# A fourth place for finished row blocks, and stores in the order of their results

## The chip, the cores and the metric

The kernel runs on one core of a Trainium2 chip. The metric is the device time of one execution in microseconds (us); the median of three executions stands for a kernel. The profile is that of one further execution, so its span is a little apart from the median. TensorE multiplies matrices, VectorE (DVE), ScalarE (ACT) and GpSimd (POOL) do the element-wise work, and SyncE (SP) issues all transfers.

## The reference

With x of 2048 rows by 512 columns, the result is a gated mixture of two branches, one gate per row:

```python
g = _sigmoid((x * gate_w).sum(-1, keepdims=True))
a = _A_ref(x, A_wqkv, A_wo)          # 32 heads of 16, causal, window of 256 rows, then @ wo
b = _B_ref(x, B_w1, B_b1, B_w2, B_b2)
return g * a + (1 - g) * b
```

Branch B works across the rows: `h = layernorm(x)`, `u = gelu(h^T w1 + b1)` with 1376 hidden columns, `y = u w2 + b2`, transposed back to 2048 by 512. Everything is bf16.

## The kernel before

The 2048 rows are 16 blocks of 128. The kernel is a list of small named tasks, each with the engines that may run it, the tasks it depends on and the buffers it takes. `PLAN` (L190 on) writes out by hand, for each engine, the order in which that engine runs its tasks; a colon and digits after a name choose the buffers that the task takes. `arrange` merges the five orders into one program, and the waits between engines follow from the data. Each engine runs its own list strictly in order, so a task that waits holds up everything behind it on its engine. SP's list is the order in which transfers are issued.

The tasks that matter here:

- `s`, `e`, `m`, `pv`: attention scores on TensorE (L904, L924), their exponential on ScalarE (L949), the window's mask on VectorE (L965, L985) or GpSimd (L518), and the product with the values on TensorE (L1010), for row block j. `n1` to `n4` (L1090 to L1125, VectorE) normalise the block and put it back into `xo`.
- `y{t}` (through `chain`, L652): 15 matmuls of 512 columns that gather row block t of the result in one PSUM bank: eleven of branch B (`ug`, `wb`) and four of branch A (`wo`, `xo`). The matmuls are handed out in pairs, so that other work lies between them. Most y blocks take turns in banks 4 and 5: y9 and the y5 after it both use bank 5.
- `f{t}` (`affine`, L420 on ScalarE, L423 on VectorE): reads that bank, multiplies by the gate and adds the bias, and writes the finished bf16 block to an SBUF buffer of the ring `otr`. The bank is free for the next y when f has ended.
- `o{t}` (L1216): SP stores that buffer to HBM, 128 KB. The buffer can be written again when the store has landed. Block 15 is cut into a left and a right half (`15l`, `15r`).
- `vz{j}` and `vs{t}` (L710, L711, L700, L701): copies of value rows from SBUF to SBUF, two transfers each, in SP's list as well.
- `gl{t}` (L804, VectorE, 12 of them, from 50.7 to 66.7 us): multiplies a row block by `gate_w`. Only the sum over the row is wanted; the products go to the tile `junk`, 128 by 512 in bf16, and are read by nobody.

`otr` has three buffers of 128 by 512 in bf16 (L397). The orders of the f and the o tasks in the plan before, with the buffer after the colon, other tasks left out:

```
VectorE:  f0:1  f4:0  f8:2  f7:0  f2:1  f9:2  f1:1  f5:0  f10:1  f11:0  f3:1  f6:1  f12:0  f14:0  f15r:1
ScalarE:  f13:2  f15l:2
SP:       o4 o0 o2 vz11 vz12 vs13 o8 o7 o1 o5 o10 vz13 o3 o11 vz14 o6 o12 o9 o13 o14 o15l o15r
```

Of the kernel before, what the change touches and what calls it, by code (L numbers as in the profile page):

```python
# [84 lines left out]
def arrange(tasks):  # L85
# [21 lines left out]
    while len(order) < len(tasks):  # L107
# [134 lines left out]
        e12.A0.0:2 e12.A0.1 e14.A0.0:9 e14.A0.1 e12.B0.0:3 e12.B0.1 e13.B1.0:6 e13.B1.1 e13.B0.0:0 e13.B0.1  # L242
        e13.A0.0:1 e13.A0.1 e13.CNone.0:7 e13.CNone.1 e14.A1.0:2 e14.A1.1 e14.CNone.0:3 e14.CNone.1 e14.B0.0:4
        e14.B0.1 e14.B1.0:1 e14.B1.1 e15.CNone.0:6 e15.CNone.1 e15.ANone.0:8 e15.ANone.1 e15.BNone.0:5 e15.BNone.1
        f13:2 f15l:2
    """,
    DVE="""
        zeros bs1:1 bs2:0 ba2 ba1 xtc0.1.0 bs3:0 bs0:1 ba0 parity ba3 const qc1_0 qc0_0 bs7:1 bs6:0 ba7 bs4:1 qc3_0
# [4 lines left out]
        n13:5 nz2:0 gl8 n40 n23 qc3_2 n4-1 gatem2 n32:0 ez1 nz3:0 n33:1 ub0 n42 n31:0 n14:6 gatem3 qc1_2 n43 ub6  # L253
        n24 kc3_3 m5.C nz4:0 qc2_2 n34:1 m6.C n44 n15:7 m6.A1 ub5 n16:3 ez2 n25 nz5:1 ub1 n35:1 m7.A0 m7.B0 kc1_3
        n26 ub4 qc0_3 m8.A0 nz6:1 m7.C n41 gates n36:0 m8.C m7.B1 n46 ub8 ub9 n17:1 kc2_3 qc2_3 kc0_3 qc3_3 n18:6
        n45 qc1_3 n28 n27 nz8:0 n38:1 nz7:1 f0:1 ez3 n48 n37:0 n47 f4:0 f8:2 m10.A0 m9.A1 m9.C f7:0 m9.B1 m9.B0
        n19:6 f2:1 n29 nz9:0 n39:0 n49 f9:2 m10.B0 m10.C m11.B1 f1:1 n110:2 n210 nz10:1 n310:0 n410 m11.A0 f5:0
        m11.A1 f10:1 n111:4 n211 nz11:1 m12.A1 n311:0 n411 m12.B1 m12.B0 f11:0 f3:1 n112:4 m13.B1 m13.B0 n212
        nz12:0 m14.A0 n312:1 m13.A0 m13.C n412 m14.A1 n113:5 f6:1 f12:0 m14.B0 n213 nz13:1 m14.B1 n313:1 n413 m15.C
        n114:0 n214 nz14:0 n314:1 n414 n115:7 n215 nz15:1 n315:1 n415 f14:0 f15r:1  # L260
    """,
    POOL="""
        ident masks pow0 ones blanks m1.B0 m0.A0 m-1.C m0.C m0.A1 m1.B1 pow2 m1.A0 pow1 m1.A1 pow3 m2.B0 m2.A1
# [3 lines left out]
    SP="""  # L267
        x0.0 x0.2 wqk0 wqk1 wqk2 wqk3 x1.4 xt1 wv x2.8 bias xt3 x3.12 vs0 w1_20 xt2 vs2 vz2:0 vs1 gw w1_10 w1_21
        w1_03 w1_00 w1_02 vz6:2 w1_01 w1_13 w1_11 w1_12 vz3:1 vz5:0 w1_22 w1_23 vz4:1 vz10:1 vz7:0 vz8:2 w2_0 w2_1
        w2_2 wo vz9:0 o4 o0 o2 vz11:0 vz12:2 vs13 o8 o7 o1 o5 o10 vz13:0 o3 o11 vz14:1 o6 o12 o9 o13 o14 o15l o15r  # L270
    """,
)

# [9 lines left out]
def kernel(  # L283
# [42 lines left out]
    wo = sb.tile([P, 4, D], BF16, name="wo")  # L326
# [38 lines left out]
    junk = sb.tile([P, D], BF16, name="junk")  # L365
# [7 lines left out]
    def ring(name, n, shape, dtype):  # L373
        return Ring(name, [sb.tile(shape, dtype, name=f"{name}{i}") for i in range(n)])
# [20 lines left out]
    ztr = ring("zt", 2, [P, D], BF16)  # L395
    rdr = ring("rd", 2, [P, 32], FP32)
    otr = ring("ot", 3, [P, D], BF16)  # L397
    vzr = Ring("vz", [VZ[:, i] for i in range(NVZ)])

    def buf(b):  # L400
        if b.ring is not ps:
            tile_ = b.ring.tiles[b.index]
            return tile_ if isinstance(tile_, bass.AP) else tile_[:]
        return pairs[b.index // 2][:] if b.size == 2 else singles[b.index][:]

    def bank(kind):
        return ps.use(1, BANKS[kind])
# [3 lines left out]
    def add(*a, **k):  # L411
        tasks.append(Task(*a, **k))
        return tasks[-1]
# [13 lines left out]
    def load(name, emit, time, lat=2.0):  # L427
        return add(name, {"SP": time}, emit, [], lat=lat)

    dx = {}  # L430
# [46 lines left out]
    def small_loads():  # L477
# [10 lines left out]
    dgw = load(  # L488
        "gw", lambda: nc.sync.dma_start(gwr[:], bass.AP(tensor=gate_w.tensor, offset=gate_w.offset, ap=[[0, P], [1, D]])),
        1.2, 2.3,  # L490
    )
# [255 lines left out]
    for i in range(NSB):  # L747
        ag = []
        for t_ in range(4 * i, 4 * i + 4):
# [7 lines left out]
                uses=[b],  # L757
# [19 lines left out]
    for i in range(NSB):  # L777
        ts = slice(4 * i, 4 * i + 4)
        if i < NGP:
            gb = bank("xt")  # L780

            def emit_gate(i=i, gb=gb):
                return [
                    nc.tensor.matmul(
                        buf(gb)[:, t_:t_ + 1], lhsT=XT[i][:, ck, t_ * P:(t_ + 1) * P], rhs=gwc[:, ck:ck + 1],
                        start=(ck == 0), stop=(ck == 3),
                    )
                    for t_ in range(4) for ck in range(4)
                ]

            gt = add(f"gate{i}", {"PE": 0.45}, emit_gate, [k3] + xt[i], takes=[gb], uses=[xts[i]], ins=32)
            gm = add(
                f"gatem{i}", {"DVE": 0.16},
                lambda gb=gb, ts=ts: nc.vector.tensor_scalar(
                    out=ez[:, ts], in0=buf(gb)[:, 0:4], scalar1=80.0, scalar2=None, op0=ALU.min,
                ),
                [gt], uses=[gb],
            )
        else:
            gt = []  # L800
            for t_ in range(4 * i, 4 * i + 4):
                gt.append(add(
                    f"gl{t_}", {"DVE": 0.72},
                    lambda t_=t_: nc.vector.scalar_tensor_tensor(  # L804
                        out=junk[:], in0=xo[:, t_, :], scalar=1.0, in1=gwr[:], op0=ALU.mult, op1=ALU.mult,
                        accum_out=ez[:, t_:t_ + 1],
                    ),
                    [dx[t_], dgw], two=True,
                ))
            lready += gt  # L810
            gm = add(
                f"gatem{i}", {"DVE": 0.16},
                lambda ts=ts: nc.vector.tensor_scalar(
                    out=ez[:, ts], in0=ez[:, ts], scalar1=80.0, scalar2=None, op0=ALU.min,
                ),
                gt, two=True,
            )
        ge = add(
            f"gatee{i}", {"ACT": 0.22}, lambda ts=ts: nc.scalar.activation(ez[:, ts], ez[:, ts], ACT.Exp), [gm]
        )  # L820
        eready.append(ge)

        def emit_spread(ts=ts, i=i):

            def move(out_, in_):
                return nc.vector.tensor_reduce(out=out_, in_=in_[:, :, None], op=ALU.add, axis=mybir.AxisListType.X)

            to = EZ[:, 16 * i:16 * i + 16].rearrange("p (t a) -> p a t", a=4)
            made = [move(to[0:32, a], ez[32 * a:32 * a + 32, ts]) for a in range(4)]
            for r in range(1, 4):  # L830
                made.append(move(EZ[32 * r:32 * r + 32, 16 * i:16 * i + 16], EZ[0:32, 16 * i:16 * i + 16]))
            return made

        zready.append(add(f"ez{i}", {"DVE": 1.25}, emit_spread, [ge]))
# [313 lines left out]
    for fc in range(NFC):  # L1148
        f0 = fc * P
# [136 lines left out]
```

The softmax here doesn't subtract the row's maximum and nothing guards it: scores larger than these inputs give would overflow.

## Time and profile before

| | before |
|---|---|
| median of three executions | 203.4 us (203.27, 203.40, 204.51) |
| the profiled execution | 201.83 us, span 200.1 us |
| TensorE busy | 193.2 us, 97% of the span |
| ScalarE, VectorE, GpSimd busy | 167.7, 155.6, 74.9 us |
| first and last f on VectorE start | 126.2 and 196.8 us |
| store of 128 KB, issue to landing | 2.4 us (median of 15) |

Times within the profile count from the start of its span. A row of the timeline is: start, duration, engine, line, operation, tiles (output<-inputs), how many instructions are merged, and in brackets how long the engine had been idle and what ended that. Matmuls overlap: the duration of a row runs to the modelled end of its last matmul, and the next row usually starts before it, so that the cost of a row of matmuls is read from start to start. "The chain that ended last" walks back from the last instruction through whatever released each step. The list of waits adds up, for each engine and line, the idle time and what ended it: total, number, longest.

### The profile page before, as it was taken

The numbers are of one execution on the slowest core, as the hardware profiler recorded it, in microseconds if no ns is written. First come the engines' busy times: TensorE is split into PE (matmuls) and PEld (weight loads), VectorE is DVE, ScalarE is ACT, GpSimd is POOL, SyncE is SP. The second block draws the span as 40 slices with busy tenths as digits, with TensorE's granted clock in tenths as the row PEclk, the third lists the DMA queues.
The fourth block names the chain that finished last, engine by engine and source line by source line (L and its number), as shares of the span: only waits on it lengthen the run. The fifth ranks groups of instructions, "written<-read, shape, count | busy, mean of one in ns | idle before, by whom it ended". The sixth has DMA issues, their size and how long they took to land.

```text
span 200.1 us, 9021 instructions
## 1 busy us (share of the span) xinstructions
PE 193.2 (97%) x4059; PEld 93.2 (47%) x4059; DVE 155.6 (78%) x289; ACT 167.7 (84%) x194; POOL 74.9 (37%) x72
## 2 busy tenths in 40 slices
PE   7899999999999999999999999999998999999993
PEld 3543344343545445446434554334545354554572
DVE  3699969989989982795779688756608986798983
ACT  3288998899898997997899799899796989998651
POOL 6494657624024479226020150202481622008120
PEclk9999999999999999999999999999999999999998
DMA  5999635996042100001199790010040011111101
GB/s 159 291 288 208 161 85 167 358 287 202 3 105 74 34 0 20 15 3 32 37 350 387 267 261 9 0 57 0 29 117 17 27 56 32 57 31 53 37 29 56
DMA packets 23189, 22.02 MB, mean 110 GB/s; under 512 B 7566, under 2 KB 21262, under 8 KB 23150
## 3 DMA queue, kind: packets, MB, share of 16 engines
q1 hardware_dynamic: 23150, 21.44, 36.0%
q8 instruction: 32, 0.52, 1.1%
q14 instruction: 7, 0.06, 0.1%
HBM read 15.61 MB, written 2.10 MB: 88 GB/s over the span
## 4 chain that ended last, share of the span: by engine, by line
PE 87%; POOL 3%; DMA 2%; ACT 2%; SPq 2%; DVE 1%; issue 1%; DVEq 0%
PE pb L652 64%; PE ps L1010 11%; PE ps L924 9%; PE ps L904 3%; POOL XT L518 3%; DMA xo<-in_A_x_dram 1%; DVE ot L423 1%; DMA out_dram<-ot 1%; ACT XT L949 1%; ACT XT L584 1%; SPq L711 1%; SPq L700 1%; SPq L710 1%; ACT et L949 1%; PE pb L590 0%
## 5 line engine op out<-in xcount | busy, mean ns | idle before, releaser
L949 ACT ACTIVATE et<-ps 128x1024 bf16<-128x1024 f32 (+1 forms) x102 | 95.9, 1001 | 13.8 <-PE ps L924 9.0
L518 POOL TENSOR_SCALAR_AFFINE_SELECT et<-et 128x1024 bf16<-128x1024 bf16 (+2 forms) x34 | 45.1, 1329 | 81.9 <-ACT et L949 48.6
L949 ACT ACTIVATE XT<-ps 128x1024 bf16<-128x1024 f32 (+1 forms) x52 | 49.4, 1011 | 4.0 <-PE ps L924 2.0
L652 PEld LDWEIGHTS <-wb 128*32 128x32 bf16 (+4 forms) x646 | 32.3, 97 | 37.1 <-issue 6.3
L652 PE MATMUL pb<-ug,wb 128*32 128x512 bf16 (+4 forms) x376 | 45.7, 369 | 0.5 <-DVE ot L423 0.5
L652 PE MATMUL pb<-h,wb 128*128 128x512 bf16 (+2 forms) x270 | 43.6, 381 | 0.0
L652 PE MATMUL pb<-XT,wqkv 128*128 128x512 bf16 (+2 forms) x184 | 32.2, 371 | 0.9 <-ACT XT L584 0.9
L518 POOL TENSOR_SCALAR_AFFINE_SELECT XT<-XT 128x1024 bf16<-128x1024 bf16 (+2 forms) x11 | 16.6, 1511 | 29.5 <-ACT XT L949 25.0
L924 PE MATMUL ps<-QZ,KT 32*128 32x256 bf16 (+1 forms) x528 | 23.9, 262 | 0.1
L1010 PEld LDWEIGHTS <-VA 128*32 128x32 bf16 (+1 forms) x1056 | 20.4, 97 | 6.9 <-issue 3.2
L736 DVE TENSOR_TENSOR QZ<-pb,par 128x1024 bf16<-128x1024 f32 x16 | 19.4, 1214 | 5.2 <-PE pb L652 5.0
L423 DVE TENSOR_SCALAR ot<-pb,c,c 128x512 bf16<-128x512 f32 (+1 forms) x15 | 11.8, 786 | 11.4 <-PE pb L652 6.5
L1010 PE MATMUL ps<-et,VA 128*32 128x128 bf16 (+2 forms) x736 | 19.2, 217 | 0.2 <-ACT et L949 0.2
L652 PEld LDWEIGHTS <-wqkv 128*128 128x128 bf16 (+1 forms) x184 | 12.3, 97 | 14.5 <-DMA wqkv<-in_A_wqkv_dram 1.1
L1090 DVE STREAM_TRANSPOSE et<-ps 128x1024 f32<-128x1024 f32 (+1 forms) x12 | 14.4, 1204 | 5.8 <-PE ps L1010 5.0
L652 PE MATMUL pb<-wo,xo 128*32 128x512 bf16 (+2 forms) x164 | 17.7, 375 | 0.0
L924 PEld LDWEIGHTS <-KT 32*128 32x128 bf16 x528 | 7.8, 92 | 20.8 <-ACT et L949 7.8
L652 PE MATMUL pb<-wqkv,XT 128*128 128x512 bf16 x64 | 16.8, 380 | 0.0
L985 DVE TENSOR_TENSOR et<-et,mask 128x1024 bf16<-128x1024 bf16 x17 | 13.2, 784 | 1.5 <-ACT et L949 1.5
L1010 PEld LDWEIGHTS <-VZ 128*32 128x32 bf16 x832 | 13.3, 98 | 0.9 <-issue 0.5
L752 DVE BATCH_NORM_STATS2 stats<-xo 128x6 f32<-128x512 bf16 x16 | 10.5, 678 | 2.6 <-DMA xo<-in_A_x_dram 2.6
L1125 DVE STREAM_TRANSPOSE xo<-zt 128x512 bf16<-128x512 bf16 (+1 forms) x17 | 11.5, 674 | 0.3
(76 smaller groups left out, 185.5 us busy)
## 6 DMA issues: line engine op xcount, KB each, us to landing
wb<-in_B_w_dram SPq DMA_DIRECT2D x8, 512.0 KB, 9.6
wb<-in_B_w_dram SPq DMA_DIRECT2D x2, 2048.0 KB, 7.9
out_dram<-ot SPq DMA_DIRECT2D x15, 128.0 KB, 2.4
VZ<-VA SPq DMA_DIRECT2D x26, 70.0 KB, 2.6
xo<-in_A_x_dram SPq DMA_DIRECT2D x3, 512.0 KB, 5.7
wb<-in_B_w_dram SPq DMA_DIRECT2D x4, 352.0 KB, 5.8
wqkv<-in_A_wqkv_dram SPq DMA_DIRECT2D x4, 256.0 KB, 4.8
wb<-in_B_w_dram SPq DMA_DIRECT2D x1, 1024.0 KB, 5.2
```

The source lines that it names most:

```text
L423: return nc.vector.tensor_scalar(out=out_, in0=in_, scalar1=scale, scalar2=bias, op0=ALU.mult, op1=ALU.add)
L518: return nc.gpsimd.affine_select(out=out_, in_=in_, pattern=[[0, n] for n in pattern] + [[step, HB]], compare_op=op, fill=0.0, base=base_, ...
L652: made.append(nc.tensor.matmul(buf(b)[c:z_, c0:c0 + w_], lhsT=lhsT[:, c:z_], rhs=rhs, start=(j == 0), stop=(j == n - 1), skip_group_check= ...
L736: lambda k=k, b=b: nc.vector.tensor_tensor(out=QZ[:, k, :, (i % NQ) * SB:(i % NQ + 1) * SB], in0=buf(b)[:, None, :].to_broadcast([P, 2, SB ...
L752: f"bs{t_}", {"DVE": 0.67}, lambda b=b, t_=t_: nc.vector.bn_stats(buf(b)[:], xo[:, t_, :]),
L904: made.append(nc.tensor.matmul(buf(b2[r // 2])[m_:m_ + HB, at:at + P], lhsT=keys(t_, k)[rows, a:a + HB], rhs=q[rows], start=True, stop=Tru ...
L924: made.append(nc.tensor.matmul(to[:, :, done:done + m], lhsT=keys(t_, k)[rows], rhs=q[rows], start=True, stop=True, tile_position=(32 * r, 0),
L949: lambda n_=n_: nc.scalar.activation(out=shape(buf(e)[:, n_ * 1024:(n_ + 1) * 1024]), in_=shape(buf(b2[n_])), func=ACT.Exp, scale=SCALE),
L985: return nc.vector.tensor_tensor(out=view, in0=view, in1=mask[:, "AB".index(x), None, :].to_broadcast([P, n_, HB]), op=ALU.mult)
L1010: return lambda: nc.tensor.matmul(to(), lhsT=v() if callable(v) else v, rhs=buf(e)[rows, col:col + n], start=first, stop=last, tile_positi ...
L1090: lambda: nc.vector.transpose(out=view(buf(tr).bitcast(FP32)), in_=view(buf(o))), [last], takes=[tr], uses=[o],
L1125: return nc.vector.transpose(out=to, in_=src)
```

## The change

The ring `otr` gets a fourth place: the tile `junk`, from when the gate's products are done. A buffer handle `jb` with index 3 is named as used by all 12 `gl` tasks, so that the planner gives the place out only after the last of them. The f tasks are spread over the four places, and the stores are put in the order in which the f tasks run; above all o0 moves ahead of o4, o8 and o7 move ahead of o2 and of the vz and vs copies, and o9 moves from behind o12 to just behind those copies. The order of the tasks on TensorE, ScalarE, VectorE and GpSimd stays, and no operation is added or taken away. The purpose is that no f has to wait for a store that is late.

```diff
 ACT
-        f13:2 f15l:2
+        f13:1 f15l:3
 DVE
-        n45 qc1_3 n28 n27 nz8:0 n38:1 nz7:1 f0:1 ez3 n48 n37:0 n47 f4:0 f8:2 m10.A0 m9.A1 m9.C f7:0 m9.B1 m9.B0
-        n19:6 f2:1 n29 nz9:0 n39:0 n49 f9:2 m10.B0 m10.C m11.B1 f1:1 n110:2 n210 nz10:1 n310:0 n410 m11.A0 f5:0
-        m11.A1 f10:1 n111:4 n211 nz11:1 m12.A1 n311:0 n411 m12.B1 m12.B0 f11:0 f3:1 n112:4 m13.B1 m13.B0 n212
-        nz12:0 m14.A0 n312:1 m13.A0 m13.C n412 m14.A1 n113:5 f6:1 f12:0 m14.B0 n213 nz13:1 m14.B1 n313:1 n413 m15.C
-        n114:0 n214 nz14:0 n314:1 n414 n115:7 n215 nz15:1 n315:1 n415 f14:0 f15r:1
+        n45 qc1_3 n28 n27 nz8:0 n38:1 nz7:1 f0:0 ez3 n48 n37:0 n47 f4:1 f8:2 m10.A0 m9.A1 m9.C f7:3 m9.B1 m9.B0
+        n19:6 f2:0 n29 nz9:0 n39:0 n49 f9:1 m10.B0 m10.C m11.B1 f1:2 n110:2 n210 nz10:1 n310:0 n410 m11.A0 f5:3
+        m11.A1 f10:0 n111:4 n211 nz11:1 m12.A1 n311:0 n411 m12.B1 m12.B0 f11:1 f3:2 n112:4 m13.B1 m13.B0 n212
+        nz12:0 m14.A0 n312:1 m13.A0 m13.C n412 m14.A1 n113:5 f6:3 f12:0 m14.B0 n213 nz13:1 m14.B1 n313:1 n413 m15.C
+        n114:0 n214 nz14:0 n314:1 n414 n115:7 n215 nz15:1 n315:1 n415 f14:2 f15r:0
 SP
-        w2_2 wo vz9:0 o4 o0 o2 vz11:0 vz12:2 vs13 o8 o7 o1 o5 o10 vz13:0 o3 o11 vz14:1 o6 o12 o9 o13 o14 o15l o15r
+        w2_2 wo vz9:0 o0 o4 o8 o7 o2 vz11:0 vz12:2 vs13 o9 o1 o5 o10 vz13:0 o11 o3 vz14:1 o6 o12 o13 o14 o15l o15r
     otr = ring("ot", 3, [P, D], BF16)
+
+    otr.tiles.append(junk)
+    otr.avail.append(None)
+    jb = Buf(otr)
+    jb.index = 3
...
-                    [dx[t_], dgw], two=True,
+                    [dx[t_], dgw], uses=[jb], two=True,
```

## The prediction

> **What bounds the kernel now.** I read the page's totals first, then the list of waits, then the chain in order of time around the one wait that the change addresses, then the timelines of TensorE and VectorE there.
>
> ```profile
> PE 193.2 (97%) x4059; PEld 93.2 (47%) x4059; DVE 155.6 (78%) x289; ACT 167.7 (84%) x194; POOL 74.9 (37%) x72
> ```
>
> TensorE is busy for 193.2 of 200.1 us; the part of the page by lines puts 87% of the final chain on it. About 3.3 us of the rest lies after its last matmul and 3 us at the start. Only a TensorE stall can be won in between. VectorE's waits from 125 us to the end:
>
> ```profile
> DVE ot L423 <- PE pb L652: 6.5, 6, 2.4
> DVE ot L423 <- DMA out_dram<-ot: 4.7, 1, 4.7
> DVE XT L1090 <- PE ps L1010: 2.4, 2, 2.0
> ```
>
> One f, and one only, waited for a store: 4.7 us. The chain in order of time shows which:
>
> ```profile
> 142.77 0.81 DVE ot L423
> 143.58 0.28 DVE XT L1094
> 143.85 0.09 SPq L1216
> ...
> 147.64 0.59 SPq L701
> 148.23 0.04 issue
> 148.28 1.92 DMA out_dram<-ot
> ...
> 150.29 0.82 DVE ot L423
> 151.11 0.05 issue
> 151.16 0.60 PE pb L652 x2
> ```
>
> The f at 142.77 is f2. SP stood in front of o2 until f2 had ended, then issued vz11, vz12 and vs13 (six transfers, 144.0 to 148.2 us), and only then o8, although f8 had run at 133.19. o8 landed at 150.2; f9 uses o8's buffer and started at 150.29; TensorE's next y (y5, in the bank that f9 reads) started at 151.16. So a store that could have gone out at 134 us held f9, and f9 held TensorE. How long TensorE stood is read from its timeline:
>
> ```profile
> 141.70 1.03 PE L652 MATMUL pb<-wo,xo 128*128 128x512 bf16 x4
> 142.57 0.59 PE L652 MATMUL pb<-ug,wb 128*128 128x512 bf16 x2
> ...
> 148.08 1.03 PE L652 MATMUL pb<-wo,xo 128*128 128x512 bf16 x4
> 149.04 0.40 PE L924 MATMUL ps<-QZ,KT 32*128 32x256 bf16 x8
> 149.37 0.39 PE L652 MATMUL pb<-ug,wb 96*128 96x512 bf16 x1
> 149.60 1.03 PE L652 MATMUL pb<-wo,xo 128*128 128x512 bf16 x4
> 151.16 0.60 PE L652 MATMUL pb<-ug,wb 128*128 128x512 bf16 x2 [0.54 <-DVE ot L423]
> ```
>
> Four such matmuls take 0.87 us from start to start when nothing holds the next (141.70 to 142.57). After 149.60 the next was due at 150.47 and came at 151.16. The bracket's 0.54 is less than the true loss of 0.69, because the matmul before is drawn to its modelled end.
>
> **What the skill says.** The page "DMA: Bandwidth & Descriptors", section "Anatomy of one DMA", says that DMA engines do not wait on semaphores: the wait is on the issuing sequencer, before dispatch. The trace agrees: o8 stood behind o2's wait on SP. The same section fits a transfer as 2.0 us fixed plus bytes over 436 GB/s, for transfers issued from GpSimd; for 128 KB this gives 2.3 us, an estimate from that page. These stores are issued by SP; the trace has a median of 2.4 us from issue to landing, and 1.92 us for o8. The page "PSUM — Partial Sum Buffer", section "PSUM bank collisions raise a hardware error", asks for semaphores between engines by bank; here that is y5 waiting for f9, 0.05 us after f9's end. The page "SBUF — State Buffer", section "Who interferes with whom", says that a VectorE instruction with two SBUF inputs and a GpSimd instruction that reads SBUF exclude one another for a whole instruction. The trace agrees: the product of L1107 took 2.52 us at 156.58, with a GpSimd mask running from 154.28 to 158.56, against 0.69 us elsewhere. This is used for a rival below.
>
> **The change part by part.**
>
> *Instructions.* None is added or removed: 15 f on VectorE at 0.81 us, 2 on ScalarE and 17 stores stay. `junk` is written by VectorE alone, and its last products end at 66.7 us; f7 writes it at about 137 us, on the same engine. Cost: none, 70 us lie between.
>
> *o8 and o7 ahead of o2, o9 behind the copies.* f9 now takes place 1, last used by f4. f4 ran from 130.04 and o4 follows it, so this place is free by about 130.85 + 2.4 = 133.3 us. f9 is then held by its input alone: y9's last matmuls are the group of four at 148.08, which ends at 148.08 + 1.03 = 149.11. With the 0.03 us that f2 took after its matmul (142.74 to 142.77), f9 starts at 149.14, 1.15 us earlier, and ends at 149.96. y5 is due at 150.47, so 0.5 us are to spare and the stall goes in full: **0.69 us**.
>
> *VectorE behind f9.* The masks m10.B0, m10.C and m11.B1 stand behind f9. In the chain pv10 is drawn in two pieces, against one for pv11:
>
> ```profile
> 152.69 1.00 PE ps L1010 x80
> 153.70 0.43 PE pb L652 x8
> 154.13 0.46 PE ps L1010 x48
> ...
> 161.53 1.36 PE ps L1010 x128
> ```
>
> pv10 took 1.00 + 0.46 = 1.46 us for the 128 matmuls that cost pv11 1.36. The timeline says why: mask m10.C (L965) ran from 151.62 for 1.22 us, to 152.84, and the first matmul that needs it started at 152.89. Shifted with f9 by 1.15 us, m10.C ends at 151.69, while that matmul will be due at 152.89 - 0.69 - 0.10 = 152.10. So another **0.10 us** go.
>
> *The other places.* Each f needs the store of the one that used its place before. f2: o0, issued at 127 instead of 131.3, needed at 142.77. f1: o8, now out at 134, needed at about 152. f5 (due 160.3): o7. f10 (161.7): o2, at 143.9 as now. f11 (170.1): o9, out at about 150. f3 (171.6): o1, at about 153. f6 and f12 (182.3): o5 and o10, by 163. f13 on ScalarE (192.0): o11, at 171. f14 (195.5): o3, at 172.5. f15l (196.3): o6, and f15r: o12, both at about 183. The closest leaves 10 us against 2.4 us: no new wait. SP's new order makes o9 wait for f9 until 150 us, with o1, o5, o10 and vz13 behind it; o1 is not ready before f1, so nothing loses. vz11, vz12 and vs13 keep their place behind o2.
>
> *What follows after 151 us.* In the chain, from 151.16 to 196.81 us every step is TensorE's own, so a TensorE that starts 0.79 us earlier ends 0.79 us earlier if the other engines follow. ScalarE is the nearest: it runs without a gap from 163.27 to 173.01. But ahead of that it waits for TensorE's scores 0.79 us at 152.28, 0.75 at 154.97 and 0.57 at 163.27, so it moves with TensorE. The masks and normalisations on VectorE are released by the two. The end (f15r for 0.55 us, two stores, about 3.3 us) is unchanged: o9 is no longer in the last burst, but it was issued early enough there.
>
> **Sum:** 0.69 + 0.10 = 0.79 us. 203.4 - 0.8 = **202.6 us**, 0.4% less.
>
> **The rivals.**
>
> *More than the profile shows.* The median lies 203.40 - 201.83 = 1.57 us above the profiled execution. I can't see where; if a later landing of o8 made all of it, the change would win 0.79 + 1.57 = 2.36 us: 201.0 us. For it: f9 to y5 is the only DMA wait on VectorE late in the kernel. Against it: the loads at the start can vary as well, and one kernel's executions lie 1.2 us apart already. The unknown is between 0 and 1.57; I take 0 and keep both for the range.
>
> *The wait only changes its name.* ScalarE, or y9 itself, sets the pace after 151 us and the 0.79 us come back as short waits for exponentials. For it: 167.7 us of ScalarE, and the gapless ten microseconds. Against it: the three waits for TensorE before those. Time: 203.4 us.
>
> *Slower.* VectorE's masks move by 1.15 us against GpSimd's, and a mask that a product awaits falls under a GpSimd mask. The held product of L1107 lost 2.52 - 0.69 = 1.83 us. All of this on TensorE's path once would give 203.4 - 0.8 + 1.8 = 204.4 us. Against it: GpSimd and VectorE both follow TensorE after 152 us, so their relation hardly moves, and the held product of today stops no matmul.
>
> **How the numbers follow.** Forecast 0.62, more than shown 0.16, only renamed 0.14, slower 0.08. The range from 201.3 to 203.8 us takes in most of the first rival, all of the second and the spread of 0.4 us or so that medians of three may have. One per cent is 2.0 us: faster means under 201.4. That needs the first rival nearly in full, 0.14. Slower means over 205.4, beyond even the slower case as worked out; I give 0.05 for two such holds. The rest, 0.81, lies within 1%.
>
> **What would show it.** In the profile after: no f waits for a store; f9 starts near 149.1, released by a matmul, with VectorE idle some 3.6 us before it instead of 4.7; the y after it starts near 150.5, with no bracket; pv10 in 1.36 us; the span near 199.3. The forecast is wrong if f9's start moves and TensorE's end does not follow by 0.7 to 0.8 us, or if a new wait for exponentials or masks stands behind 151 us in TensorE's list.

## The result and the profile after

The changed kernel took 201.63 us (median of four executions, 201.10 to 201.91), the kernel before 203.48 us (four, 203.27 to 204.51): a ratio of 0.990, 95% interval 0.9865 to 0.9935. In a later comparison on another occasion it was 201.12 against 202.86 us, ratio 0.9911 (0.9887 to 0.9935). The forecast was 202.6 us, so the change won about twice the 0.8 us that was worked out.

The page's totals after:

```profile
PE 188.7 (94%) x4025; PEld 93.5 (47%) x4059; DVE 155.8 (78%) x289; ACT 167.8 (84%) x194; POOL 74.8 (37%) x72
```

TensorE's busy time is 4.5 us less than before, but this is no gain: 34 matmuls of 4059 have no record in this trace, and TensorE's list of waits has 28 gaps, 4.4 us together, that the profile puts down to "issue"; the first trace of before has none. Starts have to be compared, not busy times. VectorE's waits from 125 us to the end:

```profile
DVE ot L428 <- PE pb L657: 5.5, 5, 2.4
DVE ot L428 <- DMA VS<-VA: 3.6, 1, 3.6
DVE XT L1095 <- PE ps L1015: 2.4, 2, 2.0
```

(Lines from about L400 on stand five further down than before.) No f waits for a store. The 3.6 us are f9's wait; this trace puts them down to a copy into `VS`, which f9 does not read. Two events ended close together, and with the same wait of 3.59 us the trace of the new order alone names the matmul (below). TensorE's timeline, then VectorE's:

```profile
148.29 1.03 PE L657 MATMUL pb<-wo,xo 128*128 128x512 bf16 x4
149.25 0.40 PE L929 MATMUL ps<-QZ,KT 32*128 32x256 bf16 x8
149.58 0.39 PE L657 MATMUL pb<-ug,wb 96*128 96x512 bf16 x1
150.02 0.81 PE L657 MATMUL pb<-wo,xo 128*128 128x512 bf16 x3
150.67 0.59 PE L657 MATMUL pb<-ug,wb 128*128 128x512 bf16 x2
```

```profile
149.35 0.81 DVE L428 TENSOR_SCALAR ot<-pb,c,c 128x512 bf16<-128x512 f32 x1 [3.59 <-DMA VS<-VA]
150.08 0.68 DVE L990 TENSOR_TENSOR XT<-XT,mask 128x1024 bf16<-128x1024 bf16 x1
150.68 1.22 DVE L970 TENSOR_TENSOR XT<-XT,mask 128x2048 bf16<-128x2048 bf16 x1
```

f9 ends at 150.16 and y5 starts at 150.67 without a bracket, four matmuls after the last branch-B matmul of y1 (one of the four has no record). In the chain in order of time, pv10 is now

```profile
152.19 0.90 PE ps L1015 x80
153.09 0.43 PE pb L657 x8
153.53 0.46 PE ps L1015 x48
```

0.90 + 0.46 = 1.36 us, the price of pv11. The chain ends with TensorE's last matmuls and the last f:

```profile
193.82 2.37 PE pb L657 x17
196.20 0.03 issue
196.22 0.54 DVE ot L428
```

From 192.7 to 193.8 us, just ahead of these rows, the profile leads the chain through a normalisation on VectorE, where the chain of before has TensorE. This is no new stop: TensorE had work there, and from 191.6 us to its end its rows stand 0.61 us earlier than before (one matmul of the group at 193.82 has no record). In the second trace of the change the chain is TensorE's own there as well.

All this is as forecast, and yet the span is 200.1 us, as in the first trace of before. Both ends differ. The first scores start 0.20 us later (12.51 against 12.31; the weights landed later), and from f15r's start to the end it takes 3.88 us instead of 3.27, because SP needed 1.22 us to issue the last but one store; another trace of the same kernel has 0.33 us there. So I compare the stretch between: from the start of the first scores to that of f15r, 196.83 - 12.31 = **184.52 us** before and 196.22 - 12.51 = **183.71 us** after. The change won 0.81 us in these two traces, by the two terms of the forecast (0.69 + 0.10).

The open question was why the times moved by 1.5 to 1.9 us and the traces by 0.8. All traces in one table; "stop" is how long TensorE stood ahead of y5, from when the matmul was due (0.87 us after the group of four) to when it came; ratios are to the kernel before. An execution more than 1.5% above the fastest of its kernel counts as slow and stays out of the ratios: one of 18 with one more copy (206.05 us) and one of four with four more (208.28 us, the traced one).

| kernel | first scores, f15r start | stretch | stop | ratio (95%) |
|---|---|---|---|---|
| before, first trace | 12.31, 196.83 | 184.52 | 0.69 | |
| before, second | 12.33, 196.96 | 184.63 | 0.75 | 0.9995 (0.9974 to 1.0015) |
| before, third | 12.06, 197.24 | 185.18 | 1.29 | |
| before, fourth | 12.30, 197.40 | 185.10 | 1.27 | |
| changed, first | 12.51, 196.22 | 183.71 | none | 0.990 (0.9865 to 0.9935) |
| changed, second | 12.17, 195.87 | 183.70 | none | 0.9911 (0.9887 to 0.9935) |
| new order, three places | 12.35, 196.12 | 183.77 | none | 0.9925 (0.9899 to 0.9951) |
| four places, old order | 12.48, 196.20 | 183.72 | none | 0.9942 (0.9902 to 0.9982) |
| o8 moved, nothing else | 12.45, 196.17 | 183.72 | none | 0.9942 (0.9914 to 0.9971) |
| last store on ScalarE | 12.39, 196.10 | 183.71 | none | 0.9924 (0.9897 to 0.9952) |
| changed, four more copies | 12.34, 196.06 | 183.72 | none | 0.9928 (0.9902 to 0.9953) |
| before, one more copy | 13.07, 198.36 | 185.29 | 1.46 | 1.0029 (1.0009 to 1.0049) |
| before, two more copies | 12.35, 199.78 | 187.43 | 2.07 | 1.0101 (1.0072 to 1.013) |
| before, four more copies | 12.98, 203.18 | 190.20 | 3.76 | 1.0174 (1.0122 to 1.0227) |

Without the wait the stretch is 183.70 to 183.77 us in seven traces. In the four traces of before it is 184.5 to 185.2 us.

### The profile page after: what moved, and what is told of

It is laid out like the page before. It is cut to its first block, busy times and chain, and to the rows that moved or that the text cites. A ratio compares the mean times of both kernels' runs of the same rounds, so it can differ in the third digit from the quotient of the medians.

```text
span 200.1 us, 8991 instructions
## 1 busy us (share of the span) xinstructions
PE 188.7 (94%) x4025; PEld 93.5 (47%) x4059; DVE 155.8 (78%) x289; ACT 167.8 (84%) x194; POOL 74.8 (37%) x72
## 4 chain that ended last, share of the span: by engine, by line
PE 86%; issue 3%; ACT 3%; POOL 3%; DMA 2%; DVE 1%; SPq 1%; DVEq 0%
PE pb L657 63%; PE ps L1015 11%; PE ps L929 9%; PE ps L909 3%; POOL XT L523 3%; DMA wqkv<-in_A_wqkv_dram 2%; ACT et L954 1%; ACT XT L954 1%; ACT VA L589 1%; SPq L441 0%; DVE XT L1095 0%; DVE ot L428 0%; SPq L457 0%; PE pb L789 0%; DVE XT L1099 0%
## 5 line engine op out<-in xcount | busy, mean ns | idle before, releaser
L657 PE MATMUL pb<-ug,wb 128*32 128x512 bf16 (+6 forms) x367 | 43.8, 369 | 1.3 <-issue 1.3
L657 PE MATMUL pb<-h,wb 128*32 128x512 bf16 (+2 forms) x260 | 41.3, 380 | 1.6 <-issue 1.6
L657 PE MATMUL pb<-XT,wqkv 128*128 128x512 bf16 (+2 forms) x176 | 30.8, 370 | 1.8 <-issue 1.1
L657 PE MATMUL pb<-wo,xo 128*32 128x512 bf16 (+2 forms) x161 | 17.1, 375 | 0.2
L428 DVE TENSOR_SCALAR ot<-pb,c,c 128x512 bf16<-128x512 f32 (+1 forms) x12 | 9.4, 781 | 9.3 <-PE pb L657 5.5
L657 PE MATMUL pb<-wqkv,XT 128*128 128x512 bf16 x60 | 15.9, 380 | 0.6 <-issue 0.5
```

Source lines behind the costliest of these rows:

```text
L428: return nc.vector.tensor_scalar(out=out_, in0=in_, scalar1=scale, scalar2=bias, op0=ALU.mult, op1=ALU.add)
L657: made.append(nc.tensor.matmul(buf(b)[c:z_, c0:c0 + w_], lhsT=lhsT[:, c:z_], rhs=rhs, start=(j == 0), stop=(j == n - 1), skip_group_check= ...
```

## The experiments

**The kernel before, unchanged.**

> The kernel before, unchanged, for the noise and for a second trace of it. The whole change measured 201.6 against 203.5 us, 1.85 us, where the one trace of before accounts for 0.8. Theory 1 (the wait of f9 for the late store was longer in the timed executions than in the profiled one): the ratio to before is 1.00, and this trace shows f9 starting later than 150.3 us, by up to 1 us more, with TensorE standing 1.7 to 2.4 us there, and a span near 201.7 us. Theory 2 (the rest of the gain comes from another place, the last burst of stores, from which o9 is gone): f9 at 150.3 as before, and the surplus lies after the last matmul, which ends near 196.8 us. Theory 3 (it lies at the start, in the loads, and is chance): the first scores start later than 12.3 us.

The ratio is 0.9995. f9 started at 150.38, the stop was 0.75 us, and the last matmuls and first scores stood where they had been. This trace supports none of the three; the kernel before was at 202.50 us here (34 executions, 201.55 to 204.58), so part of the 203.48 us of the first comparison was chance or belonged to that occasion.

**The order alone.** Three places, SP's list of the change:

```diff
-        w2_2 wo vz9:0 o4 o0 o2 vz11:0 vz12:2 vs13 o8 o7 o1 o5 o10 vz13:0 o3 o11 vz14:1 o6 o12 o9 o13 o14 o15l o15r
+        w2_2 wo vz9:0 o0 o4 o8 o7 o2 vz11:0 vz12:2 vs13 o9 o1 o5 o10 vz13:0 o11 o3 vz14:1 o6 o12 o13 o14 o15l o15r
```

> Three places with the f tasks in the places of the kernel before; only SP's list is that of the change (o0 o4 o8 o7 ahead of o2 and the copies, o9 just behind them). If the order of the stores does it all, f9 waits for its matmul only, starts near 149.1 us, and the time is that of the whole change, 201.6 us (ratio 0.99). If the fourth place is what counts, f9 still waits and the time stays at 203.4 us.

201.37 us, ratio 0.9925. The f9 row of VectorE's timeline:

```profile
149.19 0.81 DVE L423 TENSOR_SCALAR ot<-pb,c,c 128x512 bf16<-128x512 f32 x1 [3.59 <-PE pb L652]
```

f9 waits for its matmul and for nothing else; the stretch is that of the change. The fourth place is not needed for it.

**The places alone.** `junk` as fourth place, SP's list of before. Six f have other places than in the change:

```diff
     otr = ring("ot", 3, [P, D], BF16)
+    otr.tiles.append(junk)
...
-f11:1 f3:2
+f11:2 f3:3
...
-f6:3 f12:0
+f6:0 f12:2
...
-f14:2 f15r:0
+f14:0 f15r:2
```

(Where f tasks change places, the removed lines are those of the changed kernel.)

> Four places, junk as the fourth, with SP's list as in the kernel before: o8 and o7 behind the copies, o9 behind o12. f11, f3, f6, f12, f14 and f15r take other places than in the change, since a place that waits for o9 there would never come free. f9 takes the place of f4, whose store went out at 131 us, so by theory 1 the wait goes just as well: 201.6 us (ratio 0.99). By theory 2 (o9 in the last burst costs about 1 us) only 0.8 us are won: 202.6 us (ratio 0.996). If the order is what counts: 203.4 us.

201.89 us, ratio 0.9942 (0.9902 to 0.9982), which does not tell the two theories apart. The trace is clearer: f9 at 149.34 after a wait of 3.59 us for the matmul, stretch 183.72 us. Either half alone takes away the whole of f9's wait, and in the traces the two together win no more (183.71 and 183.70 us).

**One store moved.** Three places, o8 ahead of o2, all else as before:

```diff
-        w2_2 wo vz9:0 o4 o0 o2 vz11:0 vz12:2 vs13 o8 o7 o1 o5 o10 vz13:0 o3 o11 vz14:1 o6 o12 o9 o13 o14 o15l o15r
+        w2_2 wo vz9:0 o4 o0 o8 o2 vz11:0 vz12:2 vs13 o7 o1 o5 o10 vz13:0 o3 o11 vz14:1 o6 o12 o9 o13 o14 o15l o15r
```

> Three places, and one store moved in SP's list: o8 goes ahead of o2. o7 stays behind the copies and o9 behind o12. Theory 1: this one store is the whole effect, 201.6 us (ratio 0.99), f9 near 149.1 us. Theory 2: 202.6 us (ratio 0.996), since o9 is still in the last burst.

201.46 us, ratio 0.9942 (0.9914 to 0.9971); stretch 183.72 us. So one store behind six copies was the whole wait. Theory 2, which had o9 in the last burst cost the other microsecond, finds no support: here o9 is still there, and from f15r's start to the end of the span it takes 3.2 us (199.4 - 196.17), as in the first trace of before. The times alone do not exclude it: the interval takes in its 0.996, and not the 0.99 of theory 1, which rested on the 203.4 us of the first comparison. Both kernels without the wait that keep o9 late have 0.9942, the five comparisons with o9 early 0.990 to 0.9928; but on the same occasion the new order took 201.42 us on average, the places alone and the one store moved 201.58 us each, and executions of one kernel lie up to 2.2 us apart.

The traces of these kernels held a part of the answer to what was missing. SP's timeline of the first trace of before, from o2 to o8:

```profile
145.20 0.59 SPq L710 DMA_DIRECT2D VZ<-VA  x1
145.84 0.59 SPq L711 DMA_DIRECT2D VZ<-VA  x1
146.47 1.12 SPq L700 DMA_DIRECT2D VS<-VA  x1
147.64 0.59 SPq L701 DMA_DIRECT2D VS<-VA  x1
148.28 1.06 SPq L1216 DMA_DIRECT2D out_dram<-ot  x2
```

One copy takes 1.12 us to issue where the others take 0.59. In every trace one of the copies behind o2 is slow in this way: for 1.12 to 1.25 us in some, for 1.42 to 1.75 us in others. In the kernel before every tenth of that is a tenth of f9's wait; in the others nobody waits behind it. That it hits executions of before too is seen in the third trace:

```profile
145.58 1.71 SPq L711 DMA_DIRECT2D VZ<-VA  x1
147.32 0.60 SPq L700 DMA_DIRECT2D VS<-VA  x1
147.97 0.59 SPq L701 DMA_DIRECT2D VS<-VA  x1
148.60 1.06 SPq L1216 DMA_DIRECT2D out_dram<-ot  x2
```

and in what it does to TensorE there:

```profile
149.33 1.03 PE L652 MATMUL pb<-wo,xo 128*128 128x512 bf16 x4
151.49 0.61 PE L652 MATMUL pb<-ug,wb 128*128 128x512 bf16 x2 [1.13 <-DVE ot L423]
```

y5 was due at 150.20 and came at 151.49: a stop of 1.29 us. The third and fourth trace of before were taken to see this:

> The kernel before once more, for a third trace. The issue of the fourth copy behind o2 took 0.59 or 1.16 us in its two traces (with 1.12 for the fifth in the first), and 1.42 to 1.75 us in those of six other kernels. Theory 1a: f9 starts at 150.3 us or up to 0.6 us later, TensorE stands 0.7 to 1.3 us; where it stands longest, the clock may fall as behind more copies, and the span is then above 201 us. Theory 1b: as in the first two traces.

> The same, for a fourth trace. Theory 1a: one of these two shows f9 after 150.6 us. Theory 1b: neither does.

Slow copies of 1.71 and 1.69 us, stops of 1.29 and 1.27 us, f9 at 150.62 and 150.86, the clock at 1.00 around the stop: theory 1a, without the fall of the clock. These two executions took 202.92 and 202.22 us, the first two 201.83 and 201.96 us.

**Copies added ahead of o8.** One, two or four more copies of 64 rows by 512 bytes behind vs13, into `junk`; nobody reads them:

```diff
                             nc.sync.dma_start(VS[HB:P, at, :], VA[0:HB, t_, HV:H * DV + 16]),
-                        ]
+                        ] + [
+                            nc.sync.dma_start(junk[HB * (i % 2):HB * (i % 2) + HB, 256 * (i // 2):256 * (i // 2) + 256],
+                                              VA[HB * (i % 2):HB * (i % 2) + HB, t_, 0:256])
+                            for i in range(2 if t_ == NT - 3 else 0)
+                        ]
```

> The kernel before with two more copies (64 rows by 512 bytes, SBUF to SBUF, into junk, read by nobody) issued behind vs13 and so ahead of o8. A copy's issue took 0.59 us and the next began 0.05 us later, so o8 leaves 1.28 us later. Theory 1 (f9 waits for o8, and TensorE for f9, one to one): f9 starts near 151.6 us, TensorE stands 1.28 us longer, 202.5 + 1.3 = 203.8 us, ratio 1.006. Rival (the gain of the change came from elsewhere, or a longer wait is made good further on by ScalarE's slack): 202.5 to 203.0 us, ratio 1.000 to 1.002.

> The same with four more copies: o8 leaves 2.56 us later. Theory 1: f9 near 152.9 us, 202.5 + 2.6 = 205.1 us, ratio 1.013, twice the loss of two copies. Rival: under 203.5 us, ratio under 1.005.

> The kernel before with one more copy ahead of o8, 0.64 us. With two, TensorE stood from about 150.5 to 152.57 us and then ran at a granted clock of 0.50 for some three us, so that 1.3 us of wait cost 2.0 us of time; with four, 2.6 us cost 4.1. If the clock falls only after a longer stop than about 1.5 us, one copy costs 0.64 us: ratio 1.003, clock 1.00 throughout. If it falls already after a stop of 1.35 us, one copy costs 1.5 to 2 us: ratio 1.007 to 1.010. A mixture (some executions with the fall, some without) gives ratios in between and executions that lie 1 to 1.5 us apart.

| copies | added wait by their issue | ratio | cost (ratio less 1, times the 202.8 us of before) |
|---|---|---|---|
| one | 0.64 us | 1.0029 | 0.6 us (0.2 to 1.0) |
| two | 1.28 us | 1.0101 | 2.0 us (1.5 to 2.6) |
| four | 2.56 us | 1.0174 | 3.5 us (2.5 to 4.6) |

The 4.1 us for four copies in two of the expectations are the difference of the medians, 206.99 - 202.86 us. With four, f9 started at 154.02 us, not near 152.9: the first scores came 0.67 us later than in the first trace of before, and the slow copy took 1.61 us.

One copy costs what it adds: against the second trace of before, with a slow copy of nearly the same length (1.16 us there, 1.22 here), the stretch is 185.29 - 184.63 = 0.66 us longer. The wait goes one to one into the time, and nothing later makes it good. Two copies cost more than they add; for four the interval reaches down to the 2.56 us. Why, the timeline of TensorE with two copies shows:

```profile
149.63 1.03 PE L652 MATMUL pb<-wo,xo 128*128 128x512 bf16 x4
152.57 0.61 PE L652 MATMUL pb<-ug,wb 128*128 128x512 bf16 x2 [1.91 <-DVE ot L423]
153.10 0.45 PE L908 MATMUL ps<-QZ,KT 32*64 32x128 bf16 x32
153.48 0.99 PE L652 MATMUL pb<-ug,wb 128*32 128x512 bf16 x8
```

and so does the table by stretches (after the busy times of the engines, the last three columns are the granted clock, the DMA share and GB/s):

```profile
152.00:153.00 1.00, 0.43 (x2) 0.11 (x2) 1.00 (x2) 0.00 (x0) 0.00 (x0) 1.00 0.00 0
153.00:154.00 1.00, 1.00 (x41) 0.58 (x44) 1.00 (x2) 0.32 (x1) 0.00 (x0) 0.79 0.00 0
154.00:157.00 3.00, 3.00 (x107) 2.24 (x98) 1.57 (x3) 1.62 (x2) 1.31 (x1) 0.50 0.15 49
157.00:159.00 2.00, 2.00 (x66) 1.04 (x54) 1.34 (x2) 1.08 (x2) 1.95 (x2) 1.00 0.00 0
```

TensorE stood for 2.07 us (due at 150.50). It went on at full clock for one microsecond; then the granted clock fell to 0.50 until 157.0 us. From 153.6 to 157.0 us at half speed, about 1.7 us of work were lost. Against the kernel without the wait the stretch is 187.43 - 183.72 = 3.7 us longer: 2.07 for the stop and 1.6 for the clock. With one copy the stop was 1.46 us and the clock stayed:

```profile
153.00:154.00 1.00, 1.00 (x42) 0.52 (x44) 1.00 (x2) 0.20 (x1) 0.00 (x0) 1.00 0.00 0
154.00:157.00 3.00, 3.00 (x153) 2.13 (x144) 2.49 (x4) 2.25 (x3) 1.19 (x1) 1.00 0.15 48
```

In the same 3 us TensorE did 153 matmuls instead of 107. The two executions differ in where they stand in the work by a fraction of a microsecond; the clock makes the difference.

The length of the stop does not settle alone whether the clock falls. In the trace with four copies TensorE stood for 3.76 us, from when the matmul was due (151.13) to 154.89, and the clock fell while it stood (busy TensorE, then the same last three columns):

```profile
153.00:154.00 1.00, 0.00 (x0) 1.00 0.74 261
154.00:155.00 1.00, 0.11 (x1) 0.56 0.01 1
155.00:156.00 1.00, 1.00 (x16) 0.50 0.00 0
159.00:161.00 2.00, 2.00 (x72) 0.51 0.09 27
161.00:165.00 4.00, 4.00 (x38) 1.00 0.01 4
```

But another of the four executions took 205.18 us at a mean clock of 1.00: 2.4 us more than before, about the 2.56 us of the copies, and no fall. And with one copy two of 18 executions (204.42 and 204.82 us) have a mean clock of 0.992, where two copies have 0.990 to 0.992, so the clock probably fell in them too; no trace shows how long TensorE stood there.

**The same copies in the changed kernel.** Four more copies behind vs13, into `gwr` (its last reader has long run):

> The changed kernel with the four more copies behind vs13 (into gwr, which nobody reads any more at that time, since junk is now in use). In the kernel before they cost 4.1 us. If they cost this only by standing ahead of o8, they cost nothing here: o9 leaves 2.6 us later and f11 needs it at 170 us; f9 near 149.3 us, 201.1 to 201.4 us, ratio to before 0.991 to 0.994. If the copies or the fuller queue cost time in themselves, 202 us or more.

201.14 us, ratio 0.9928; f9 at 149.19, stretch 183.72 us. The copies in themselves cost nothing. They cost 3.5 us only where a store that somebody waits for stands behind them.

**The changed kernel again, and a store on ScalarE.**

> The changed kernel, unchanged, beside these, for more executions of it. From f15r's start less the first scores' start the traces give 184.5 and 184.6 us before and 183.7 after: 0.85 us. Theory 1a (the trace of before shows a short case: the six copies ahead of o8 took 4.2 to 4.3 us there, and up to 4.9 us in the traces of kernels in which nothing waits for them): about 1.2 us, 201.3 us, ratio 0.994. Theory 1b (the traces of before are typical and the first comparison was high by chance): 0.8 us, ratio 0.996. Both have f9 near 149.3 us; only the time tells them apart, if it does.

201.12 us, ratio 0.9911; the interval (0.9887 to 0.9935) excludes the 0.996 of theory 1b, and even the 0.994 of theory 1a lies just outside it: the mean gain of an execution is larger than the first traces of before have it.

```diff
-                lambda ot=ot, t_=t_, c0=c0, c1_=c1_: nc.sync.dma_start(
+                lambda ot=ot, t_=t_, c0=c0, c1_=c1_, tag=tag: (nc.scalar if tag == "l" else nc.sync).dma_start(
```

(with o15l at the end of ScalarE's list instead of in SP's)

> The changed kernel with the store of the left half of block 15 issued by ScalarE, behind the f15l that makes it, instead of by SP ahead of the right half's store. In the traces of the changed kernel and of the new order alone SP needed 1.22 and 1.26 us for that issue, in four others 0.46 to 0.55. If that is SP's own business, the last store goes out as soon as f15r has ended, the stretch from f15r's start to the end of the span is 3.1 us in all executions, and the time is 0.1 to 0.6 us under the changed kernel's: 201.0 us. If the two issues hinder each other wherever they come from, it stays at 201.3 to 201.6 us.

201.16 us, ratio 0.9924, against 201.12 us of the changed kernel beside it: no gain that these runs show. The issue took ScalarE 0.37 us, and from f15r's start to the end of the span it was 3.1 us (199.2 - 196.10); the changed kernel beside it had 3.0 us (198.9 - 195.87), with 0.33 us for the issue on SP. The slow issue of 1.22 us did not come in either trace, so whether ScalarE avoids it is open.

## Why the prediction was right, and where it fell short

The direction, the range (201.3 to 203.8 us) and the mechanism held; the gain was undersized by a half, and the range held because most of the first rival had been taken into it.

*The stop of TensorE, 0.69 us.* The step was right for the execution that the trace showed, down to the instant: f9 at 149.14 was forecast, 149.35 less the late start of 0.20 is 149.15; y5 was due at 150.47, and 150.67 less 0.20 is 150.47. This is the term that was mis-sized. Two of the four traces of before have stops of 0.69 and 0.75, two have 1.29 and 1.27; the mean is 1.00 us. The step took the wait of one execution for that of all, and in it the 1.12 us that one of the copies needed, though its five neighbours needed 0.5 to 0.6.

*pv10, 0.10 us.* Right: 1.46 us became 1.36.

*No cost of the places and of the new order, no new wait.* Right: in seven traces without the wait, with three or four places and three orders of the stores, the stretch agrees within 0.07 us. (By the times that the forecast lists, the closest place leaves 13 us and not 10; nothing hangs on it.)

*What follows after 151 us.* Right. TensorE's end moved by as much as the stop was shorter, and one more copy moved it back one to one. ScalarE followed; the rival in which the wait only changes its name is refuted by the same two facts.

*Slower.* Refuted. VectorE's product beside the GpSimd mask was still held at that place (2.52 us before, 2.61 in both traces of the change), and still stopped no matmul.

*More than the profile shows.* This rival, at 0.16, was partly right, by the mechanism that it names, a later landing of o8: o8 does leave up to 0.6 us later in some executions. It was not the whole 1.57 us between the median and the profiled execution.

*What stays open.* The means of the stretches give 184.86 - 183.72 = 1.1 us for the change; the ratios of the seven comparisons without the wait give 1.2 to 2.0 us, 1.5 on average. The intervals of five of the seven reach down to 1.1 us; those of the changed kernel itself do not (1.3 us). A fall of the clock in executions of before does not close the gap: with two copies the mean clock of an execution came down to 0.990 to 0.992, while of the 84 executions of before in the later comparisons none is under 0.996, and the 0.997 of its first trace comes from the end, where the clock is at 0.50 from 199 us on, behind the last matmul. What is missing lies with the kernel before: its four traced executions took 202.23 us on average, the 64 that stand beside the later experiments 202.75 us, while the two traced ones of the change took 201.27 us and all eight on record 201.31 us. Four executions can lie low by chance, or longer stops than 1.29 us occur in some without a trace; which of the two it is stays open.

## What to carry to other kernels

On a queue in which transfers are issued in order, ask of each transfer who waits for its landing, and what stands ahead of it; a store that frees a buffer belongs ahead of copies whose first reader runs 17 us later (vz11, issued at 144.04 us, is first read by pv11 at 161.6), and in the traces one line moved was worth as much as a fourth buffer and a new order. A wait that one trace shows is one draw: where its length holds a step that is irregular among its neighbours, look at the same step in further traces before the sum is made. And a stop of TensorE can cost more than its length: the one of 2.07 us lost another 1.6 us to the clock, those of up to 1.46 us lost nothing more in the traces.

## What of the hardware was unexpected

The granted clock of TensorE fell to 0.50 in the traces with two and with four more copies. Both times it fell 2.8 to 2.9 us after TensorE's last matmul had ended: from 150.66 to 153.6 us with two copies, when work had gone on for one microsecond after a stop of 2.07 us, and from 151.29 to 154.1 us with four, while TensorE still stood. It came back after 3.4 us in the first and 6.8 us in the second; in the first the price was 1.6 us. After stops of 1.29 and 1.46 us it stayed at 1.00. But one execution with four copies kept a mean clock of 1.00, though its stop must have been some 3.2 us (an estimate: the 0.69 us of the first trace of before and the 2.56 us of the copies). The Trainium skill, page "TensorE: Matmul & The Clock Gate", section "Part 1: The HAM clock gate", describes such a gate with half the clock as its lower state, which agrees, and names about 3.4 us of idling as what brings it down. Here 2.07 us were enough in one execution, and the measurement decides.

The issue of a transfer on SP is not of one length. In this program the copies of 64 rows from SBUF to SBUF take 0.5 to 0.6 us, the stores 0.33 us and up, but in every trace one of the copies behind o2 took 1.1 to 1.75 us, and the last but one store of the program took 0.33 us in one execution and 1.22 in another. What holds it is not seen.
